# A gated attention and MLP mix on one core: POOL's subtractions go to VectorE, the gelu table is loaded first, a normalisation moves between other products

## The chip, the core and the metric

The kernel runs on one core of a Trainium2 chip. Its engines work side by side, each through its own queue in order: TensorE (PE; its weight loads are listed as PEld), VectorE (DVE), ScalarE (ACT), GpSimd (POOL) and SyncE (SP), which issues most of the DMAs. The metric is the device time of one execution in microseconds (us), lower is better.

## The reference

The input x has 2048 tokens of 448 features, in float32. Two branches are mixed by a gate per token.

```python
g = sigmoid((x * gate_w).sum(-1, keepdims=True))
# A: attention, 16 heads of 28, one k and one v for all heads
q, k, v = x @ wq, x @ wk, x @ wv
o = softmax(q @ k.T * 28 ** -0.5) @ v        # per head
a = o @ wo
# B: MLP
h  = gelu(layernorm(x) @ w1)                 # gelu by tanh
hs = shift(h) @ w2                           # the four quarters of h, shifted by +1, -1, +2, -2 tokens
x1 = x + hs
b  = x1 + gelu(layernorm(x1) @ w3) @ w4      # 448 -> 1792 -> 448
out = g * a + (1 - g) * b
```

## The kernel before

Float32 values are multiplied as two float32r parts: for each weight and activation there is a high part (wh, ah), which ACT makes by a cast, and a low part (wl, al), which is the raw value less the high part. A product takes three matmuls (high by high, high by low, low by high; L115 to L119 in proj). So every matrix that PE reads has had a subtraction made for it on DVE or POOL.

The work is done in blocks of 512 tokens (four blocks, b = 0 to 3), each of four tiles of 128 tokens (t). The stages:

1. Ahead of the MLP. For each block: k, v and the gate's sum from x (stage_kv, stage_v; stage_v transposes vT on PE and DVE copies the result into vext and gz), q for the first two head groups (stage_q), the first layernorm, the w1 product with gelu (stage_w1), the w2 product (stage_w2), which is added to x1. layernorm_stats makes mean and variance by bn_stats on DVE (L126, L127) and rs, the inverse deviation, by two small instructions on POOL (L128, L129). layernorm_tile makes xn on DVE (L135), a pad of 64 columns that repeats its last 64 (L137, on POOL), four transposes on PE (L140), and the split into ah and al (split_a: ACT L109, DVE L110 and L111). In stage_w1 ACT computes gelu twice from PSUM, once into hh (the high part) and once into hf; hl, the low part, is hf less hh, made on POOL (L306). hf has two buffers, xn three, the PSUM tiles mm two, tp two, misc and mx one each.
2. The MLP's weights. load_w34(i), for i = 0 to 6, loads 256 columns of w3 and 256 rows of w4 through one raw buffer each and splits them; the low part of w4 is made on POOL (L371). Before, the first is called ahead of stage_w2(2) and the next three ahead of stage_w2(3). The rest follow behind it.
3. The MLP. Its layernorm of block 0 (ln_begin, ln_tile) lies between the tiles of stage_w2(3); later ones lie within the preceding block. For f = 0 to 13, PE computes 128 columns of w3's product (g), ACT two gelus (gh L409, gf L410), DVE the low part gl (L411), and PE multiplies by w4, two steps later (L419 to L421). DVE adds the sums to x1 (L449).
4. The gate: Exp on ACT (L456), then three small DVE instructions make gg, the gate, and gi, one less the gate.
5. Attention, over 16 units u (four head groups of four token blocks, 16 key tiles kt each, so 256 steps k). Per step there are four score matmuls (L663), four Exps on ACT (L665), and, two steps later, four products with v (L625). Between them lie the q products of later units (q_job), the maxima of scores, the normalisation (norm_job) and the wo products (wo_job), which end in gate_out (L564): out = gg * wo + x1, where x1 has been multiplied by gi on POOL ahead of that (L596, 16 instructions of 128x448).

The order on PE is written out by hand: it runs in the order in which the program issues its instructions (manual_schedule for PE). On the other engines and on the DMA queues a planner orders the instructions when the kernel is built: by its own costs it issues what is ready, in program order among what is ready, and the queue then keeps that order, also where the chip is later or earlier than planned. The planner also places the tables of ACT's functions: a table load (ACT_TABLE_LOAD) comes ahead of an instruction whose function isn't in the table that is loaded.

The lines that the steps of the prediction touch, besides those printed below:

```python
nc.scalar.copy(w4h[i], raw)                                              # L370, ACT
nc.gpsimd.tensor_tensor(w4l[i], raw, f32(w4h[i]), ALU.subtract)          # L371, POOL
stage_w2(NB - 2)                                                         # L386
stage_v(3, vT)                                                           # L387
for i in range(1, 4):
    load_w34(i, s2a)                                                     # L389
ln_tile(0, 0, misc_tile)                                                 # L390
stage_w2(NB - 1, lambda t: ln_tile(0, t + 1, (misc_tile, max_tile)[t % 2]) if t < 3 else None)
```

Of the kernel before, what the change touches and what calls it, by code (L numbers as in the profile page):

```python
# [8 lines left out]
F32 = mybir.dt.float32  # L9
F32R = mybir.dt.float32r  # L10
AF = mybir.ActivationFunctionType
ALU = mybir.AluOpType
# [3 lines left out]
P = 128  # L16
S = 2048
D = 448
# [3 lines left out]
C = D // 4  # L22
NB = S // 512
# [12 lines left out]
def f32(ap):  # L36
    return ap.bitcast(F32)
# [3 lines left out]
def gated_mix_kernel(  # L41
# [33 lines left out]
    sel8 = keep.tile([P, P], F32R, name="sel8")  # L75
    mcs = [keep.tile([P, P], F32R, name=f"mc_{i}") for i in range(2)]
    nc.gpsimd.memset(epst, EPS)
    nc.gpsimd.memset(powt, -0.5)
    nc.gpsimd.memset(vext, 0.0)
# [12 lines left out]
    def misc_tile(name):  # L92
        return psA.tile([P, 512], F32, tag="misc", bufs=1, name=name)

    wps = misc_tile("warm_ps")
    for _ in range(30):
# [35 lines left out]
    def layernorm_tile(pool, tp_of, b, t, mv, rs, ah, al):  # L132
        xt = x1[:, 4 * b + t, :]
        xn = pool.tile([P, 512], F32, tag="xn", bufs=3, name=f"xn_{pool.name}_{b}_{t}")
        nc.vector.tensor_scalar(xn[:, 0:D], xt, mv[:, t, 0:1], rs[:, t:t + 1],  # L135
                                op0=ALU.subtract, op1=ALU.mult)
        nc.gpsimd.tensor_copy(xn[:, D:512], xn[:, 384:D])  # L137
        tp = tp_of(f"tp_{pool.name}_{b}_{t}").rearrange("p (c n) -> p c n", c=4)
        for c in range(4):
            nc.tensor.transpose(tp[:, c, :], xn[:, c * P:(c + 1) * P], ident)  # L140
        cols = slice(t * P, (t + 1) * P)
        split_a(tp, ah[:, :, cols], al[:, :, cols])
# [60 lines left out]
    with tc.tile_pool(name="s1b", bufs=1) as s1b, \  # L203
# [89 lines left out]
        def stage_w1(b):  # L293
# [4 lines left out]
            for m in range(4):  # L298
                ps = mm_tile(f"h_{b}_{m}")
                proj(ps[0:C, :], w1h[:, :, m * C:(m + 1) * C], w1l[:, :, m * C:(m + 1) * C], *acts[b][0:2])  # L300
                if b + 1 < NB:
# [3 lines left out]
                nc.scalar.activation(hf[0:C, :], ps[0:C, :], AF.Gelu_apprx_tanh)  # L305
                nc.gpsimd.tensor_tensor(hl[b][0:C, m, 2:514], hf[0:C, :], f32(hh[b])[0:C, m, 2:514],  # L306
                                        ALU.subtract)
# [23 lines left out]
        vT = stage_kv(0)  # L331
        split_w(wqraw, wqh, wql, nc.gpsimd)
        stage_q(0)
# [3 lines left out]
        for t in range(4):  # L337
            ln1_tile(0, t)
        split_w(w1raw, w1h, w1l, nc.gpsimd)
        stage_w1(0)  # L340
        nc.scalar.copy(w2h[0:C], w2raw[0:C])
        nc.gpsimd.tensor_tensor(w2l[0:C], w2raw[0:C], f32(w2h)[0:C], ALU.subtract)
        stage_w1(1)
# [16 lines left out]
        def load_w34(i, pool):  # L360
# [9 lines left out]
            nc.scalar.copy(w4h[i], raw)  # L370
            nc.gpsimd.tensor_tensor(w4l[i], raw, f32(w4h[i]), ALU.subtract)  # L371

# [7 lines left out]
        def ln_tile(b, t, tp_of):  # L380
            ah, al, mv, rs = acts[b]
            layernorm_tile(s2a, tp_of, b, t, mv, rs, ah, al)

        ln_begin(0)
        load_w34(0, s2a)
        stage_w2(NB - 2)  # L386
        stage_v(3, vT)  # L387
        for i in range(1, 4):
            load_w34(i, s2a)  # L389
        ln_tile(0, 0, misc_tile)  # L390
        stage_w2(NB - 1, lambda t: ln_tile(0, t + 1, (misc_tile, max_tile)[t % 2]) if t < 3 else None)

# [61 lines left out]
    with tc.tile_pool(name="s3", bufs=1, reuse_waits="tile") as s3, \  # L454
            tc.tile_pool(name="ps3", bufs=1, space=PSUM, reuse_waits="tile") as ps3:
        nc.scalar.activation(gg, gz, AF.Exp, scale=-1.0)  # L456
        nc.vector.tensor_scalar(gg, gg, 1.0, None, op0=ALU.add)
# [136 lines left out]

        for n in range(NT):
            nc.gpsimd.tensor_scalar(x1[:, n, :], x1[:, n, :], gi[:, n:n + 1], None, op0=ALU.mult)  # L596

        jobs = []
# [47 lines left out]
        for k in range(NU * NT + LAG):  # L646
# [7 lines left out]
            if k < NU * NT:  # L654
                if kt == (7 if u == 0 else 2) and u + 2 < NU:
                    jobs.insert(0, lambda u=u: q_job(u + 2))
                if kt == 8 and (u + 3) % NG == 0 and u + 3 < NU:
                    load_x((u + 3) // NG)
                p_of[k] = []
                for j in range(4):  # L660
# [149 lines left out]
```

## Time and profile before

| | |
|---|---|
| median of 3 runs | 1070.5 us (1069.8 to 1071.85) |
| profiled execution | 1070.98 us, span 1069.1 us |
| mean granted TensorE clock | 0.987 |
| busy, share of the span | PE 97%, ACT 63%, PEld 64%, DVE 24%, POOL 15% |
| instructions | PE 5610, DVE 521, ACT 1318, POOL 182 |
| table loads on ACT | 5, of 1.283 us each: at 1.19, 26.14, 117.96, 138.38 and 417.95 us |
| stages | up to 132 us: stage 1 and the first weights; 132 to 424: the MLP; from 424: attention |

A row of the timeline gives the start and the duration in us, the engine, the line in the kernel, the operation, what it writes and reads with the shape, how many instructions are merged in it, and in brackets the time that the engine idled before it and what ended that. An x2 row's duration is that of both. Clock shares are those that the throttle granted (1.00 is full speed).

### The profile page before, as it was taken

What the parts mean: (1) busy time and instruction counts of PE and PEld (TensorE: products, weight loads), DVE (VectorE), ACT (ScalarE), POOL (GpSimd) and SP (SyncE); (2) the same over time, 40 slices, a digit from 0 to 9 for tenths busy, and PEclk for the clock granted to TensorE, in tenths of its full rate; (3) what the DMA queues carried; (4) which work ended last, traced back from release to release, by engine and by line L of the source; (5) the groups of instructions that cost most, each with busy time, mean ns of one, the idle gap of its engine ahead of it and who ended that gap; (6) DMA issues with size and microseconds to landing.
All of it is one profiled execution on the core that took longest, in us unless ns stands there. A gap on an engine that the chain in (4) does not pass through costs nothing.

```text
span 1069.1 us, 13948 instructions
## 1 busy us (share of the span) xinstructions
PE 1039.7 (97%) x5610; PEld 679.6 (64%) x5610; DVE 258.0 (24%) x521; ACT 673.2 (63%) x1318; POOL 159.8 (15%) x182
## 2 busy tenths in 40 slices
PE   6999889999999999999999999999999999999995
PEld 4787778888888888454554555554655555555542
DVE  6744952311411311401110110120110210111102
ACT  5444451222222223788888888889888889888873
POOL 5622430110200201603000002010002100000100
PEclk9999899999999999999999999999999999999998
DMA  9401330000000000423211202220202220211001
GB/s 312 131 1 37 111 111 1 1 1 1 1 1 1 1 1 29 164 32 70 33 17 16 31 20 40 39 31 3 39 10 41 39 31 2 40 24 26 10 2 38
DMA packets 30541, 41.15 MB, mean 38 GB/s; under 512 B 8004, under 2 KB 20100, under 8 KB 30340
## 3 DMA queue, kind: packets, MB, share of 16 engines
q1 hardware_dynamic: 30324, 40.04, 16.3%
q8 instruction: 46, 0.75, 0.3%
q14 instruction: 27, 0.22, 0.1%
q10 hardware_dynamic: 144, 0.13, 0.1%
HBM read 23.28 MB, written 3.67 MB: 25 GB/s over the span
## 4 chain that ended last, share of the span: by engine, by line
PE 91%; DVE 4%; DMA 1%; ACT 1%; POOL 1%; issue 1%; SPq 0%; POOLq 0%; ACTq 0%; DVEq 0%
PE s L663 27%; PE pv L625 22%; PE acc L420 4%; PE acc L419 4%; PE acc L421 4%; PE g L115 4%; PE g L116 4%; PE g L117 4%; PE q L503 3%; PE m L166 2%; PE wo L560 1%; PE wo L558 1%; PE wo L556 1%; PE g L119 1%; PE g L118 1%; PE h L116 1%
## 5 line engine op out<-in xcount | busy, mean ns | idle before, releaser
L665 ACT ACTIVATE p<-s 128x512 f32<-128x512 f32 x1024 | 517.6, 627 | 98.1 <-PE s L663 97.8
L663 PE MATMUL s<-qs,kS 98*128 98x512 f32 x1024 | 343.6, 420 | 1.4 <-ACT p L665 0.7
L663 PEld LDWEIGHTS s<-qs,kS 98*128 98x128 f32 x1024 | 181.6, 189 | 168.2 <-ACT p L665 127.1
L625 PE MATMUL pv<-p,vext 128*32 128x512 f32 x2048 | 247.6, 602 | 0.0
L409 ACT ACTIVATE gh<-g 128x512 fp32r<-128x512 f32 x56 | 33.6, 600 | 174.9 <-PE g L119 174.9
L625 PEld LDWEIGHTS pv<-p,vext 128*32 128x32 f32 x2048 | 53.7, 109 | 107.6 <-issue 100.3
L411 DVE TENSOR_TENSOR gl<-gf,gh 128x512 fp32r<-128x512 f32 x56 | 41.3, 738 | 192.1 <-ACT gf L410 192.0
L419 PE MATMUL acc<-w4h,gh 128*128 128x448 f32 x224 | 82.6, 369 | 0.0
L420 PE MATMUL acc<-w4l,gh 128*128 128x448 f32 x224 | 82.0, 366 | 0.0
L421 PE MATMUL acc<-w4h,gl 128*128 128x448 f32 x224 | 81.7, 365 | 0.0
L167 DVE TENSOR_REDUCE mr<-m 128x4 f32<-128x512 f32 x64 | 44.3, 692 | 146.0 <-PE m L166 145.3
L548 POOL CAST onh<-on 128x512 fp32r<-128x512 f32 x15 | 9.2, 614 | 414.8 <-DVE on L545 228.7
L115 PE MATMUL g<-ah,w3h 128*128 128x512 f32 x168 | 67.1, 399 | 3.1 <-ACT gf L410 2.8
L116 PE MATMUL g<-al,w3h 128*128 128x512 f32 x168 | 66.5, 396 | 0.1
L117 PE MATMUL g<-ah,w3l 128*128 128x512 f32 x168 | 66.3, 394 | 0.0
L521 DVE SCALAR_TENSOR_TENSOR good<-rt,good 128x16 f32<-128x16 f32 x15 | 2.6, 175 | 190.2 <-DMA rt<-o 190.2
L419 PEld LDWEIGHTS acc<-w4h,gh 128*128 128x128 f32 x224 | 42.0, 188 | 4.9
L420 PEld LDWEIGHTS acc<-w4l,gh 128*128 128x128 f32 x224 | 42.1, 188 | 4.8
L421 PEld LDWEIGHTS acc<-w4h,gl 128*128 128x128 f32 x224 | 42.0, 188 | 3.6
L166 PEld LDWEIGHTS m<-kS,qs 96*128 96x128 f32 x256 | 38.4, 191 | 6.3 <-DVE mr L167 1.2
L115 PEld LDWEIGHTS g<-ah,w3h 128*128 128x128 f32 x168 | 31.9, 190 | 9.7 <-ACT gf L410 3.3
L564 DVE SCALAR_TENSOR_TENSOR ot<-wo,gg,x 128x448 f32<-128x448 f32 x16 | 10.9, 682 | 108.0 <-PE wo L560 108.0
(204 smaller groups left out, 1144.4 us busy)
## 6 DMA issues: line engine op xcount, KB each, us to landing
qs<-qh SPq DMA_DIRECT2D x32, 256.0 KB
qs<-ql SPq DMA_DIRECT2D x16, 256.0 KB
xq<-in_xT_dram SPq DMA_DIRECT2D x4, 1024.0 KB
x<-in_x_dram SPq DMA_DIRECT2D x4, 896.0 KB
w3raw<-in_w_dram SPq DMA_DIRECT2D x7, 512.0 KB
out_dram<-ot SPq DMA_DIRECT2D x16, 224.0 KB
w4raw<-in_w_dram SPq DMA_DIRECT2D x7, 448.0 KB
xkv<-in_xT_dram SPq DMA_DIRECT2D x3, 1024.0 KB
```

The costliest lines, as they stand in the source:

```text
L115: nc.tensor.matmul(ps, wh[:, c, :], ah[:, c, :], start=(c == 0), stop=False)
L116: nc.tensor.matmul(ps, wh[:, c, :], al[:, c, :], start=False, stop=False)
L117: nc.tensor.matmul(ps, wl[:, c, :], ah[:, c, :], start=False, stop=False)
L166: nc.tensor.matmul(ps[:, j, :], q_of[u][0:96, j, t * P:(t + 1) * P], kS[0:96, 0:MK], start=True, stop=True)
L167: nc.vector.reduce_max(mx_of[u][:, :, t], ps, axis=AX.X)
L411: nc.vector.tensor_sub(gl, gf, f32(gh))
L419: nc.tensor.matmul(ps, gh[:, tok], w4h[i][:, k, :], start=(f == 0), stop=False)
L420: nc.tensor.matmul(ps, gh[:, tok], w4l[i][:, k, :], start=False, stop=False)
L421: nc.tensor.matmul(ps, gl[:, tok], w4h[i][:, k, :], start=False, stop=(f == NF - 1))
L625: nc.tensor.matmul(pv[32 * j:32 * j + 32, :], vext[:, kt, :], ps[j], start=(kt == 0), stop=(kt == NT - 1), tile_position=(0, 32 * j))
L663: nc.tensor.matmul(ps, kS[0:98, kt * P:(kt + 1) * P], q_of[u][0:98, j, :], start=True, stop=True)
L665: nc.scalar.activation(p, ps, AF.Exp, scale=SCALE)
```

## The change

The change has six parts.

- All subtractions that POOL makes ahead of attention go to DVE: the low parts of wq (in two halves of 128 columns), w1, w2, w4, and hl. The pad in layernorm_tile is no longer a copy on POOL; DVE computes it from x1 as a second, 64 columns wide instruction of the same kind as xn's.
- A gelu of four columns is issued on ACT at the start, from a constant tile, so that ACT's first table is gelu's.
- The MLP's layernorm of block 0 lies between the tiles of stage_w2(2) instead of stage_w2(3): stage_v(3) after the first tile, then ln_tile(0, 0) to (0, 2) after the following ones, and ln_tile(0, 3) ahead of stage_w2(3). All use the tp banks instead of misc and mx.
- load_w34(1) to (3) stand behind stage_w2(3) in the program.
- The gate's Exp takes a bias, a zero that DVE computes from x1's last tile (max with 0, then min with 0), so it can't run before x1 is complete.
- The 16 multiplications of x1 by gi stand in unit 1 of the attention, one per key tile, instead of ahead of it.

```diff
@@ kernel's start
+    zero = keep.tile([P, 4], F32, name="zero")
+    nc.gpsimd.memset(powt, -0.5)
     nc.gpsimd.memset(epst, EPS)
-    nc.gpsimd.memset(powt, -0.5)
...
+    nc.scalar.activation(zero, powt, AF.Gelu_apprx_tanh)
     wps = misc_tile("warm_ps")
@@ layernorm_tile
-        nc.vector.tensor_scalar(xn[:, 0:D], xt, mv[:, t, 0:1], rs[:, t:t + 1],
-                                op0=ALU.subtract, op1=ALU.mult)
-        nc.gpsimd.tensor_copy(xn[:, D:512], xn[:, 384:D])
+        for lo, hi, at in ((0, D, 0), (384, D, D)):
+            nc.vector.tensor_scalar(xn[:, at:at + hi - lo], xt[:, lo:hi], mv[:, t, 0:1], rs[:, t:t + 1],
+                                    op0=ALU.subtract, op1=ALU.mult)
@@ stage_w1
-                nc.gpsimd.tensor_tensor(hl[b][0:C, m, 2:514], hf[0:C, :], f32(hh[b])[0:C, m, 2:514],
+                nc.vector.tensor_tensor(hl[b][0:C, m, 2:514], hf[0:C, :], f32(hh[b])[0:C, m, 2:514],
                                         ALU.subtract)
@@ order of the stages
-        split_w(wqraw, wqh, wql, nc.gpsimd)
+        for u in range(2):
+            w = slice(u * P, (u + 1) * P)
+            split_w(wqraw[:, :, w], wqh[:, :, w], wql[:, :, w])
...
-        split_w(w1raw, w1h, w1l, nc.gpsimd)
+        split_w(w1raw, w1h, w1l)
         stage_w1(0)
         nc.scalar.copy(w2h[0:C], w2raw[0:C])
-        nc.gpsimd.tensor_tensor(w2l[0:C], w2raw[0:C], f32(w2h)[0:C], ALU.subtract)
+        nc.vector.tensor_tensor(w2l[0:C], w2raw[0:C], f32(w2h)[0:C], ALU.subtract)
@@ load_w34
-            nc.gpsimd.tensor_tensor(w4l[i], raw, f32(w4h[i]), ALU.subtract)
+            nc.vector.tensor_tensor(w4l[i], raw, f32(w4h[i]), ALU.subtract)
@@ ahead of the MLP
         load_w34(0, s2a)
-        stage_w2(NB - 2)
-        stage_v(3, vT)
+        stage_w2(NB - 2, lambda t: ln_tile(0, t - 1, tp_tile) if t else stage_v(3, vT))
+        ln_tile(0, 3, tp_tile)
+        stage_w2(NB - 1)
         for i in range(1, 4):
             load_w34(i, s2a)
-        ln_tile(0, 0, misc_tile)
-        stage_w2(NB - 1, lambda t: ln_tile(0, t + 1, (misc_tile, max_tile)[t % 2]) if t < 3 else None)
@@ the gate
-        nc.scalar.activation(gg, gz, AF.Exp, scale=-1.0)
+        nc.vector.tensor_scalar(zero[:, 0:1], x1[:, NT - 1, 0:1], 0.0, 0.0, op0=ALU.max, op1=ALU.min)
+        nc.scalar.activation(gg, gz, AF.Exp, scale=-1.0, bias=zero[:, 0:1])
@@ attention
-        for n in range(NT):
-            nc.gpsimd.tensor_scalar(x1[:, n, :], x1[:, n, :], gi[:, n:n + 1], None, op0=ALU.mult)
...
+                if u == 1:
+                    nc.gpsimd.tensor_scalar(x1[:, kt, :], x1[:, kt, :], gi[:, kt:kt + 1], None, op0=ALU.mult)
```

## The prediction

> **What bounds the kernel now.** I read the page's busy rows first (PE busy 97%), then the busy time by stretch, PE's waits up to 170 us, and the timeline around each of those waits. The profiled execution took 1070.98 us (span 1069.1 and 1.9 around it), 0.5 over the median of the runs shown, 1070.5.
>
> The busy time by stretch (columns: length, then PE, PEld, DVE, ACT, POOL busy, PE clock, DMA share, GB/s):
>
> ```profile
> 10.00:42.34 32.34, 23.30 (x102) 16.65 (x102) 27.02 (x64) 16.93 (x27) 21.48 (x29) 0.89 0.96 280
> ...
> 104.58:132.34 27.76, 24.79 (x118) 21.89 (x116) 24.82 (x51) 13.68 (x22) 12.89 (x17) 0.88 0.42 128
> 132.34:147.27 14.93, 12.01 (x45) 9.53 (x46) 8.63 (x16) 9.16 (x15) 8.15 (x10) 0.89 0.48 139
> ```
>
> ```profile
> 170.00:400.00 230.00, 229.76 (x1091) 199.51 (x1090) 54.27 (x98) 55.64 (x103) 21.08 (x23) 1.00 0.00 1
> ```
>
> In the MLP (170 to 400) PE idles 0.24 us in 230: nothing that another engine does there is worth anything. Attention is the same (PE's waits after 425 us add up to under 3 us). What can be won lies in the first three stretches, where PE waits and its granted clock is below 1. PE's longest waits up to 170 us:
>
> ```profile
> PE g L115 <- ACT gf L410: 2.8, 1, 2.8
> PE tp_s2a L140 <- DVE gz L276: 2.7, 1, 2.7
> PE h L116 <- DVE al L110: 1.9, 2, 1.6
> ```
>
> The timeline (start, duration) shows what stands behind them:
>
> ```profile
> 26.47 3.99 POOL L342 TENSOR_TENSOR w2l<-w2raw,w2h 112x1792 fp32r<-112x1792 f32 x1
> 27.10 4.04 DVE L135 TENSOR_SCALAR xn_s<-x,mv_s,rs_s 128x448 f32<-128x448 f32 x2
> ```
>
> ```profile
> 117.96 1.28 ACT L456 ACT_TABLE_LOAD   x1
> 118.02 2.42 POOL L371 TENSOR_TENSOR w4l<-w4raw,w4h 128x896 fp32r<-128x896 f32 x1 [3.71 <-ACT w4h L370]
> 118.42 2.31 DVE L105 TENSOR_TENSOR w3l<-w3raw,w3h 64x256 fp32r<-64x256 f32 x1
> ```
>
> ```profile
> 137.43 0.94 ACT L370 CAST w4h<-w4raw 128x896 fp32r<-128x896 f32 x1 [1.91 <-DMA w4raw<-in_w_dram]
> 138.38 1.28 ACT L409 ACT_TABLE_LOAD   x1
> 139.68 0.60 ACT L409 ACTIVATE gh<-g 128x512 fp32r<-128x512 f32 x1
> 140.17 0.59 ACT L410 ACTIVATE gf<-g 128x512 f32<-128x512 f32 x1
> ```
>
> A DVE instruction on SBUF operands that meets a POOL subtraction ends only when that ends: two of L135, 0.51 each elsewhere, take 4.04; L105, 0.41 elsewhere, takes 2.31. DVE reads of PSUM are not held (L148 at 17.22 took 0.68 beside L104 on POOL). And the gate's Exp (L456), issued in the middle of the gelu work, costs two table loads; the second lies ahead of the first gelu of the MLP, for which PE waits from 138.0 to 140.82.
>
> **Part 1, the first 42 us.** The chain that ended last runs through DVE here (10.99 to 42.34). Added to DVE in this stretch, with durations of its own rows: wq01l in two halves, 128x384 as L110 (0.56) and 64x128 as L111 (0.29); the first half falls into DVE's idle time before 10.99, the second counts, 0.85. w1l: 128x1344 lies between L104 at 768 (0.94) and L110 at 1536 (1.75), 1.55; 64x448 between 0.41 and 0.69, 0.62; together 2.2. w2l at 1792 columns: 2.0, past the last row by the same slope. hl: 0.69 (L411) for three, 2.1. The pads: 128x64 lies between L457 (128x16, 0.15) and L275 (128x112, 0.27), I take 0.19; eight, 1.5. Sum 8.6. Taken away: the stall of L135, 4.04 - 1.02 = 3.0. The remaining 5.6 have two places to go: DVE idles 32.34 - 27.02 = 5.3 here (3.75 of it behind POOL's rs), and 6.9 of its work is ahead of need (eight bn_stats with their aggregates and three xn from 31.06 on, for blocks 2 and 3). PE also loses two waits: q L117 on POOL's wq01l (1.2), which goes over into the wait for vT that follows, so 0; and the transposes behind the pads, which POOL's w1l held from 17.1 to 20.0 (1.0 of PE's time), which go over into DVE's queue. From al at 27.06 to 42.34 PE takes 15.3; at full clock four blocks cost 4 x (11 x 0.231 + 0.44) = 11.9, so at most 3.4 can come out there. I take a gain of 1.0, between 3 gained and 4 lost. The gelu table loaded at once is worth 0: the load that goes (26.14, 1.28) lies in ACT's wait of 3.98 for h, and the first load lies ahead of the first weights (ACT waits for them until 3.90).
>
> From 42 to 104 us PE hardly waits and DVE is busy 26 to 58% of each ten us; thirteen more hl and eight pads (10.5 us) fit. But hf has two buffers: a late hl holds ACT's next hf, and behind that hh, ah and the PSUM bank for h. That is a rival below.
>
> **Part 2, the normalisation between the w2 products.** Before, 104.58 to 132.34 takes 27.76 us. Its matmuls at full clock: 96 of w2 at 0.2035 (19.5), four groups of transposes at 0.44 (1.8), the v transposes 0.3: 21.6. The 6.1 beyond are the wait of 2.7 at 117.77 (the misc bank was held until DVE, late through L135's 3.15 beside POOL's w4l, had copied vp away), 12 matmuls at 0.37 instead of 0.20 after it (2.0), and small ones. With the change vp no longer shares its bank with the transposes, and the fourth transposes have a whole w2 block (9.8 us) behind them before g needs them. New waits: vp now comes after the first token tile, at 107.0, and vT is ready at 107.3 (0.3). The first transposes then come up at 107.6 + 2.44 = 110.1; xn follows rs, which ended at 110.8, so with the pad it is there at 111.6: a wait of 1.5. Behind it stand all of PE's later products. Together 23.4, a gain of 4.4, of which I take off 0.4 for an hl and a w4l ahead of xn in DVE's queue: 4.0 (6 if the statistics come early, 1 if DVE holds xn back for longer).
>
> **Part 3, the start of the MLP.** PE reaches g four us earlier, at 128.3, and ends two blocks (22 x 0.231) at 133.4. It then waits for ACT's gf. In ACT's queue before stands the cast w4h of the fifth weight load ahead of the first gelu (137.43, quoted above), waiting for its transfer; I take that order as kept. That cast is paced by a round: transfer 3.3 to 3.5, w4h 0.94, w4l on POOL 2.1, next transfer (127.54 to 134.01: 6.5). With w4l on DVE, 1.08 by the slope above, a round takes 5.45. From w4l of load 0 ending at 111.6 and a first transfer of 4.1, w4h of load 1 starts at 115.7 and that of load 4 at 132.1, with a us of queueing per two rounds at 133.5. No table load follows; gh and gf end at 135.5, and the third block starts there instead of 140.82: 5.3 earlier in all, 4.0 of it from part 2, 1.3 from here. The wait left is about 2: waits up to 1.6 (vp, 13.8) left the clock at 1, 2.7 and 2.8 did not; the slow matmuls after 140.82 cost 1.4, of which I count half, 0.7. Gain of part 3: 2.0, between 0 and 4.2 (the whole wait and the slow clock).
>
> Beside the load at 138.38 the Trainium skill speaks: its page "ScalarE: Activation LUTs", section "What ACT_TABLE_LOAD costs", puts 1.28 us for the load and another 1.38 for a drain at each switch. The trace shows the load of 1.28 starting 0.01 after the cast's end and gh 0.02 after the load's: no drain. By the page the sum would come out 1.4 lower; I go by the trace.
>
> **Part 4, attention.** The gate's Exp now waits for x1 of the last tile: L449 ends at 424.76, the new max/min on DVE about 0.15 (L457), so at 425.0 the Exp (0.22) can run; the first p starts at 424.38. If it is queued behind the first p it costs 0.3, if ahead of it 0.85; behind it stand all p, which PE waits for until 430. If it is queued later, 0. I take 0.3 lost. The table load stays covered (417.95, 5.1 before the first p). The sixteen products x1 x gi (1.43 each, 22.9) move past POOL's memsets, wql, ahq and onh into the second head group: there POOL has 22.9 + 6.7 (ahq, alq) + 1.9 (onh, onl) = 31.5 of about 39 us; their first reader is gate_out two groups later: 0. The pads in the MLP: 0, its PE never waits.
>
> **Sum:** -1.0 - 4.0 - 2.0 + 0.3 = -6.7 on 1070.98: 1064.3; on the median of the runs, **1063.8**. A measurement of this kernel can tell 0.2%, 2.1 us, from no change.
>
> **Rivals.**
> Gelu first (0.25): the planner puts the first gelu ahead of the late weight casts. For it: PE comes four us earlier. Against: the weights come earlier too, by about the same. Part 3 then gives 4.2: 1061.6.
> Weights ahead (0.15): with rounds of 5.45 one more w4h gets ahead of the first gelu, and the wait grows by a round: 1069.2. For it: ACT's queue before already has one cast out of place.
> Table stays (0.07): the max/min is folded or the Exp is still early, and the load remains at 138.38: 1.3 back, 1065.1.
> DVE becomes the bound (0.08), the slower side: up to 64 us DVE gets 8.6 + five hl (3.4) + four pads (0.8) = 12.8 for 3.0 taken away, and hl stands in the queue ahead of al, through which ACT and PE stall. For it: DVE is busy 27.02 of 32.34 already, and in order. Against: 6.9 of that is ahead of need. If all 9.8 stay on the path: +9.8 - 4.0 - 2.0 + 0.3 = +4.1, 1074.6. It decides from 7.8 us on (5.7 and the 2.1).
>
> **Chances.** Forecast 0.45, the rivals as given. Faster: 0.45 + 0.25 + 0.07 and a third of "weights ahead" with an early gain in part 1, 0.05: 0.82. Within 0.2%: the rest of that one, 0.10. Slower 0.08. The range takes in part 1 at its better end with "gelu first" on the low side (1061.6 - 2, then part 2 at its better end, 1058), and "weights ahead" on the high side, 1069.5.
>
> **What would show it.** Right: no L135 or L105 over 1 us before 424; three table loads (gelu, Exp, at most one more), none between 30 and 400; g starting some 5 us earlier against the first h; PE's wait at the third g block near 2 us, none for gz. Wrong: PE waits for al or hf longer than 2 us between 20 and 60; DVE over 95% busy there; a w4h cast waiting for its DMA ahead of the first gh.

## The result: slower by 1.2%

The changed kernel takes 1084.44 us (median of 4 runs, 1082.79 to 1085.35) against 1071.17 of the kernel before in the same series: ratio 1.0123, interval 1.0104 to 1.0141. The forecast was 1063.8. The profiled execution took 1084.56 us, span 1082.8, 13.7 more than before.

I cut both traces at the same events on PE, so that each part of the prediction has its own row (us; "third w2" is the start of the third block of w2 products, "first acc" of the first product with w4, s and pv are the first scores and the first product with v).

| stretch | before | after | difference | forecast |
|---|---|---|---|---|
| start to third w2 (part 1) | 104.58 | 109.25 | +4.7 | -1.0 |
| third w2 to first g (part 2) | 27.76 | 25.68 | -2.1 | -4.0 |
| first g to first acc (part 3) | 12.51 | 7.52 | -5.0 | -2.0 |
| first acc to first s (the MLP) | 279.09 | 280.02 | +0.9 | 0 |
| first s to first pv | 6.42 | 7.00 | +0.6 | +0.3 |
| first pv to the end of the span | 638.74 | 653.33 | +14.6 | 0 |
| sum | | | +13.7 | -6.7 |

One row decides the sign. PE's longest waits over the whole span, after the change:

```profile
PE q L507 <- POOL alq L493: 12.1, 1, 12.1
PE vp L275 <- ACT vT L269: 3.1, 1, 3.1
PE h L118 <- DVE al L112: 3.0, 2, 1.8
PE tp_s2a L142 <- DVE xn_s2a L138: 2.6, 2, 2.4
```

The wait of 12.1 did not exist before, nor is there a wait for gf at the third g any more. What POOL did meanwhile stands in its timeline after the change:

```profile
424.72 11.29 POOL L661 TENSOR_SCALAR x<-x,gi 128x448 f32<-128x448 f32 x7 [7.86 <-DVE gi L463]
435.98 1.84 POOL L586 TENSOR_TENSOR wql<-wqraw,wqh 128x768 fp32r<-128x768 f32 x1
...
440.96 8.31 POOL L661 TENSOR_SCALAR x<-x,gi 128x448 f32<-128x448 f32 x6
449.23 3.42 POOL L493 TENSOR_TENSOR alq<-xq,ahq 128x1536 fp32r<-128x1536 f32 x1
```

Thirteen products of x1 and gi (L661) run ahead of alq, the low part of the x that the q product of unit 2 reads. In the kernel before, twelve of the sixteen ran inside the MLP, in fours from 211.57, 282.95 and 354.34; the other four ran between 423.03 and 430.27, and none stood between wql and alq:

```profile
423.03 2.79 POOL L596 TENSOR_SCALAR x<-x,gi 128x448 f32<-128x448 f32 x2 [62.91 <-DVE x L449]
...
427.48 2.79 POOL L596 TENSOR_SCALAR x<-x,gi 128x448 f32<-128x448 f32 x2
...
437.35 3.49 POOL L489 TENSOR_TENSOR alq<-xq,ahq 128x1536 fp32r<-128x1536 f32 x1 [1.32 <-DVE ahq L488]
```

So alq ran at 437.35 before and runs at 449.23 now. PE's order is fixed, and from 440.6 on it stands at that q. The same stretch by tens of us (length, PE, PEld, DVE, ACT, POOL busy, PE clock, DMA share, GB/s):

```profile
430.00:440.00 10.00, 10.00 (x52) 4.55 (x45) 2.48 (x4) 6.86 (x15) 10.00 (x7) 0.79 0.00 0
440.00:450.00 10.00, 0.59 (x3) 0.15 (x1) 0.10 (x1) 2.34 (x5) 10.00 (x9) 0.72 0.28 92
450.00:460.00 10.00, 7.29 (x32) 3.85 (x33) 0.73 (x2) 1.60 (x4) 9.82 (x7) 0.60 0.32 107
```

POOL is busy for ten of ten us and PE for 0.59 from 440 to 450. In the ten us in which PE resumes (at 452.7) its clock is 0.60: a group of 16 pv takes 3.64 at 454.18 and took 1.92 at 435.93. Of the 14.6 us the wait is 12.1; the slow clock around it is the likely home of the other 2.5 (an estimate: the granted clock is 0.58 from 452.7 to 459.0, and 6.3 x 0.42 is 2.6).

The first three stretches after the change (same columns):

```profile
10.00:42.34 32.34, 24.58 (x100) 17.91 (x98) 28.14 (x69) 14.66 (x25) 4.18 (x5) 0.79 0.99 278
109.25:134.93 25.68, 22.65 (x118) 19.78 (x117) 22.22 (x51) 11.67 (x20) 2.52 (x8) 1.00 0.42 140
134.93:142.45 7.52, 7.52 (x34) 6.19 (x33) 6.75 (x16) 4.26 (x8) 1.77 (x4) 1.00 0.42 136
```

In the first, POOL fell from 21.48 to 4.18 us, DVE rose by only 1.1, and the clock fell from 0.89 to 0.79. In the second and third the clock is now 1.00 (before, 0.88 and, up to 147.27, 0.89), and the third has no idle PE at all: the start of the MLP went better than forecast.

### The profile page after: what moved, and what is told of

Same layout as the page of the kernel before. It is cut to its first block, busy times and chain, and to the rows that moved or that the text cites. A ratio compares the mean times of both kernels' runs of the same rounds, so it can differ in the third digit from the quotient of the medians.

```text
span 1082.8 us, 13947 instructions
## 1 busy us (share of the span) xinstructions
PE 1042.7 (96%) x5610; PEld 680.8 (63%) x5610; DVE 275.5 (25%) x584; ACT 670.5 (62%) x1319; POOL 109.8 (10%) x123
## 4 chain that ended last, share of the span: by engine, by line
PE 89%; DVE 3%; DMA 2%; POOL 2%; ACT 2%; issue 0%; SPq 0%; DVEq 0%; ACTq 0%; POOLq 0%
PE s L666 26%; PE pv L626 22%; PE acc L422 4%; PE acc L423 4%; PE acc L424 4%; PE g L117 3%; PE g L118 3%; PE g L119 3%; PE q L507 3%; PE m L168 2%; PE wo L564 1%; PE wo L562 1%; PE wo L560 1%; PE g L121 1%; PE g L120 1%; DMA w1raw<-in_w_dram 1%
## 5 line engine op out<-in xcount | busy, mean ns | idle before, releaser
L414 DVE TENSOR_TENSOR gl<-gf,gh 128x512 fp32r<-128x512 f32 x56 | 38.6, 692 | 179.6 <-ACT gf L413 179.5
L168 PE MATMUL m<-kS,qs 96*128 96x128 f32 x256 | 36.4, 265 | 0.4 <-DVE mr L169 0.4
```

Of the source, the lines that this page charges most:

```text
L168: nc.tensor.matmul(ps[:, j, :], q_of[u][0:96, j, t * P:(t + 1) * P], kS[0:96, 0:MK], start=True, stop=True)
L414: nc.vector.tensor_sub(gl, gf, f32(gh))
```

## Experiments on attention: what puts the products first

In the kernel before, 12 of the 16 products had run inside the MLP. The change did two things to them: it wrote them later (in unit 1), and it held the gate's Exp, so that gi is made only at 424.35. The first experiment writes them ahead of attention again and keeps the held Exp.

```diff
@@ a1_loop_back: from the changed kernel
+        for n in range(NT):
+            nc.gpsimd.tensor_scalar(x1[:, n, :], x1[:, n, :], gi[:, n:n + 1], None, op0=ALU.mult)
...
-                if u == 1:
-                    nc.gpsimd.tensor_scalar(x1[:, kt, :], ...)
```

> The changed kernel, with the 16 products x1 * gi written ahead of attention again, as in the kernel before. Theory H (the gate's Exp, held until x1 is complete, makes all 16 products ready at once at attention's start, and the planner fills POOL's waits with them, wherever the program writes them): POOL's queue stays the same, PE waits about 12 us for alq near 440, total 1084.5 +- 1.5. Theory W (writing them into unit 1 is what put them there): the wait goes, total about 1070.

Measured: 1086.22 us, ratio 1.0129 (1.0108 to 1.0151), PE's wait for alq 14.1: theory H, with a total a little above its range. From the first pv to the end it takes 653.3 us, as long as the changed kernel, so where the products are written makes no difference to attention; the total is longer because third w2 to first g takes 28.0 here. The second takes the hold from the Exp and leaves the products in unit 1.

```diff
@@ a2_exp_early: from the changed kernel
-        nc.scalar.activation(gg, gz, AF.Exp, scale=-1.0, bias=zero[:, 0:1])
+        nc.scalar.activation(gg, gz, AF.Exp, scale=-1.0)
```

> The changed kernel with the gate's Exp free again (no zero as its bias); the products x1 * gi stay in unit 1. Theory H: most of the 16 products are done within the MLP, no PE wait for alq over 1 us, attention 14 us shorter; the Exp goes back into the gelu work with two table loads, which costs 0 to 4 us at the MLP's start: total 1070 to 1074. Theory W: the wait for alq stays, total 1084 or more.

Measured: 1070.37 us, ratio 0.9985 (0.9971 to 0.9999); the wait for alq is 1.4 (theory H: under 1), the table loads are back at 112.73 and 136.67, and first s to first pv is 6.4 again. The third keeps the held Exp and makes gi wait for the maxima of unit 1 (they are multiplied by zero and added), so the products can't be ready when POOL still has alq to do.

```diff
@@ a3_gi_late: from the changed kernel, in unit 1 at kt == 0
+                        nc.vector.tensor_scalar(gi, gg, -1.0, 1.0, op0=ALU.mult, op1=ALU.add)
+                        nc.vector.scalar_tensor_tensor(gi, late_of[1], 0.0, gi, op0=ALU.mult, op1=ALU.add)
```

> The changed kernel with gi made to wait for the score maxima of unit 1 (gi gets 0 times the maxima added), so that the products are ready only some 30 us into attention. The Exp stays held. Theory H: no PE wait for alq, all 14 us come back, total 1070 +- 1 and attention's first score matmul at about 422.5 as in the changed kernel. Rival: POOL's wql and alq are late for another reason (casts on VectorE, the transfer): PE still waits some us there, total over 1074.

Measured: 1069.69 us, ratio 0.9981 (0.9968 to 0.9994). POOL's timeline of this kernel:

```profile
436.04 3.47 POOL L494 TENSOR_TENSOR alq<-xq,ahq 128x1536 fp32r<-128x1536 f32 x1 [1.31 <-ACT p L672]
...
442.69 4.06 POOL L598 TENSOR_TENSOR wol<-woraw,woh 128x1792 fp32r<-128x1792 f32 x1
447.49 22.12 POOL L665 TENSOR_SCALAR x<-x,gi 128x448 f32<-128x448 f32 x16 [0.74 <-DVE gi L664]
```

All 16 follow alq, woh and wol, and PE waits for none of them. So the loss of some 15 us is the meeting of two things: the held Exp makes all 16 products of 1.43 ready at the start of attention, and the planner, which takes what is ready, puts thirteen of them ahead of alq. That the hold does it is shown by the three runs; why the planner took thirteen is not. On the chip DVE had made wqh and ahq by 431.98, and wql and alq are 8.6 us of work on POOL; by an estimate they could have ended near 440.5, where PE comes to its q. The order was fixed before that by the planner's own costs, which no run shows. Everything below is built on a3_gi_late, so that attention is out of the way.

## Experiments on the first 105 us: four moves that do not add

First each of the four moves to DVE was undone alone, then all four together. For these kernels I count from the first q product, because that start varies by up to a us between executions; the columns split at the first transposes (tp) of the first layernorm.

```diff
@@ b1_wq_pool
+        split_w(wqraw, wqh, wql, nc.gpsimd)          # in place of two halves on DVE
@@ b2_w12_pool
+        split_w(w1raw, w1h, w1l, nc.gpsimd)
+        nc.gpsimd.tensor_tensor(w2l[0:C], w2raw[0:C], f32(w2h)[0:C], ALU.subtract)
@@ b3_hl_pool
+                nc.gpsimd.tensor_tensor(hl[b][0:C, m, 2:514], hf[0:C, :], ...
@@ b4_pad_pool
+        nc.gpsimd.tensor_copy(xn[:, D:512], xn[:, 384:D])   # in place of the second DVE instruction
@@ b5_all_pool: all four (w4l stays on DVE, the normalisation where the change has it)
```

> As the one with gi late, and the low part of wq back on POOL in one piece; the rest of stage 1 stays on VectorE. Theory C (the earlier wq part only made PE end its first q product sooner, so that its wait for vT grew from 1.6 to 3.2 us, over the point at which the clock is lowered, and the second q product ran slow): the wait for vT is 1.6 to 2.0 again, the first transposes start near 18.3 instead of 19.3 to 20.5, and the third w2 block starts 1 to 2 us before the 108.9 of the one with gi late. Rival Q (VectorE's queue alone sets this stage): 0 to 0.8 us earlier.

> As the one with gi late, and the low parts of w1 and w2 back on POOL (4.2 us less on VectorE). Theory Q (VectorE's queue): the third w2 block starts 1 to 3 us before 108.9. Rival S (they cost VectorE as much on POOL, by holding its instructions: 3 us before): no more than 0.7 us earlier.

> As the one with gi late, and hl back on POOL. Theory Q: 2.8 us less on VectorE in each block of stage 1; the first h of the second block waits under 1.2 us for al instead of 2, without the slow clock after it, and the third w2 block starts 1.5 to 3 us before 108.9. Rival (hl is done in VectorE's waits): under 0.7 us earlier.

> As the one with gi late, and the pads back on POOL. Theory Q: 0.2 to 0.3 us less on VectorE for each of them, eight up to the second block: the third w2 block starts 0.5 to 2 us before 108.9. Between the w2 products the first transposes' wait for the pad (2.4) shrinks to about 1.2, since on POOL the pad isn't queued behind w3l and w4l: another 1.2 us. Rival (the pads lie in waits): no gain before 109.

> As the one with gi late, and besides that all of stage 1 back on POOL: low parts of wq (in one piece), w1, w2, hl and the pads; w4's low part stays on VectorE, and the new order of the normalisation too. Theory D (VectorE's longer queue cost the 4.7 us up to 109 us of the changed kernel): the third w2 block starts at 104.6 +- 0.7 again, total 1065 to 1067. If the pads on POOL hold the transposes between the w2 products, 1 to 2 us of that are lost. Rival (the loss there comes from the gelu table at the start or from the order of the DMAs): the third w2 block stays at 109, total 1070.

Then the reverse: one move alone on DVE, the other three on POOL (b5_all_pool with one of the edits above taken out).

```diff
@@ d1_wq_dve: b5_all_pool without b1's edit      d2_w12_dve: without b2's
@@ d3_hl_dve: without b3's                       d4_pad_dve: without b4's
```

> b5_all_pool with the one move of wq01l (two halves of 128x384 and 64x128) to DVE; w1l, w2l, hl and the pads stay on POOL. In b5_all_pool the third w2 block starts at 104.58, with all four moves on DVE (a3_gi_late) at 108.90. Theory 'own time': each move costs its share of those 4.3 us by its DVE time of part 1 (0.85 of 8.6): third block at 105.0. Theory 'gap and clock': q of unit 0 ends earlier while vT does not, PE waits about 3 for vT, its clock falls, and the first transposes start near 20.5 instead of 18.1: 2.3 later, of which DVE's queue, without the other three moves, gives little back: third block at 106 to 107. Theory 'filled queue': a single move falls into DVE's idle time: 104.6. Total time 1066.6 plus the same difference.

> b5_all_pool with w1l and w2l on DVE, the rest of part 1 on POOL. Theory 'own time': 4.2 of 8.6, so 2.1 later: third block at 106.7. Theory 'filled queue': DVE is given 4.2 us of its own and rid of the 3.0 in which POOL's w2l held two xn, 1.2 net, and its 5.3 us of idle time takes that: 104.6, or up to 1 earlier (103.6), since the pads no longer lie behind POOL's w1l, which cost PE 1.0 before. Theory 'gap and clock': PE's wait for vT stays at 1.6 and the transposes start at 18.1: nothing is lost before the first h.

> b5_all_pool with hl on DVE, the rest of part 1 on POOL. Theory 'own time': 2.1 of 8.6 up to 42 us, 1.1 later: third block at 105.6. Theory 'filled queue': 2.1 us fall into 5.3 of idle time: 104.6. Theory 'filled queue, with holds': hl stands on DVE ahead of al of the next block, and POOL's pads and w2l hold it; each hl held for one POOL operation costs up to 1 us: 106 to 107 and PE waits for al at h.

> b5_all_pool with the pads on DVE, the rest of part 1 on POOL. Theory 'own time': 1.5 of 8.6 up to 42 us, 0.75 later: third block at 105.3. Theory 'filled queue': the pads fall into idle time, and the transposes no longer wait for the pads behind POOL's w1l (1.0 of PE's time before): 103.6 to 104.6. In part 2, where b5_all_pool takes 24.9 from the third w2 block to the first g, a pad of token tile 0 queued on DVE behind w3l and w4l would add up to 0.8 (25.7).

| kernel | on DVE | q to tp | tp to third w2 | both | ratio to before (interval) |
|---|---|---|---|---|---|
| before | none | 8.89 | 86.20 | 95.1 | 1 |
| b5_all_pool | none | 8.82 | 86.46 | 95.3 | 0.9959 (0.9943 to 0.9976) |
| a3_gi_late | all | 10.40 | 89.56 | 100.0 | 0.9981 (0.9968 to 0.9994) |
| b1_wq_pool | all but wq | 8.84 | 91.01 | 99.9 | 0.9988 (0.9971 to 1.0004) |
| b2_w12_pool | all but w1, w2 | 11.65 | 92.08 | 103.7 | 1.0019 (1.0005 to 1.0033) |
| b3_hl_pool | all but hl | 11.63 | 91.13 | 102.8 | 1.0016 (0.9995 to 1.0037) |
| b4_pad_pool | all but pads | 11.61 | 88.48 | 100.1 | 0.9999 (0.9988 to 1.0011) |
| d1_wq_dve | wq | 9.76 | 85.85 | 95.6 | 0.9949 (0.9935 to 0.9963) |
| d2_w12_dve | w1, w2 | 9.89 | 89.91 | 99.8 | 1.0002 (0.9988 to 1.0015) |
| d3_hl_dve | hl | 8.86 | 87.50 | 96.4 | 0.9961 (0.9944 to 0.9979) |
| d4_pad_dve | pads | 10.39 | 94.50 | 104.9 | 1.0038 (1.0022 to 1.0054) |

All four together cost 4.7; alone they cost 0.3, 4.5, 1.1 and 9.6, in sum 15.5; and undoing any one of them gives nothing back. One trace stands behind each row, so small differences need a measure. Six kernels have none of the four on DVE (before, b5_all_pool and the four others of the next section): they take 95.1 to 95.7. Four have all of them there (the changed kernel, a1, a2 and a3): 98.8 to 100.2, with a first column of 8.3 to 11.3. So the 0.3 of wq can't be told from nothing, and the 1.1 of hl hardly; in total time, too, d1 and d3 are level with b5_all_pool. "Own time" fails for w1 and w2 and for the pads, and so does the theory that a single move falls into DVE's idle time (it holds for wq and nearly for hl alone). Where the cost is large, it is in who stands beside whom and ahead of whom. In b2_w12_pool, DVE and then POOL:

```profile
15.89 5.36 DVE L138 TENSOR_SCALAR xn_s<-x,mv_s,rs_s 128x448 f32<-128x448 f32 x5 [1.44 <-POOL rs_s L131]
...
31.40 5.70 DVE L138 TENSOR_SCALAR xn_s<-x,mv_s,rs_s 128x448 f32<-128x448 f32 x6 [1.41 <-POOL rs_s L131]
```

```profile
15.82 3.05 POOL L106 TENSOR_TENSOR w1l<-w1raw,w1h 128x1344 fp32r<-128x1344 f32 x1
...
31.33 4.00 POOL L348 TENSOR_TENSOR w2l<-w2raw,w2h 112x1792 fp32r<-112x1792 f32 x1
```

Five xn and pads, 1.80 elsewhere, take 5.36 because POOL's subtraction began 0.07 earlier. With the pads on POOL, as in b5_all_pool, POOL has a pad to copy ahead of w1l, and w1l starts at 16.50, when the first three xn are nearly done (15.52 to 16.88). d4_pad_dve has the same rows of 5.36 and 5.69 as b2_w12_pool, and PE's waits of 4.2 and 4.1 behind them. The Trainium skill, page "SBUF — State Buffer", section "SBUF: two separate sides", calls the port pair that DVE and GpSimd share "an exclusive lock, not a bandwidth split", held by the first for its whole instruction. These rows agree (POOL's two pieces of w1l end at 20.13, the five on DVE at 21.25), and so does the other direction: POOL's rs, 0.20 alone, took 1.89 at 29.15 after the change, beside DVE's w2l of 1.99 at 28.98. The forecast looked at only one direction.

d2_w12_dve has no xn held by POOL and loses 4.5 all the same. (It has one hold the other way, three pads on POOL that take 2.52 at 16.89 beside w1l on DVE; that may be part of its longer first column.) DVE and then POOL:

```profile
17.59 1.55 DVE L106 TENSOR_TENSOR w1l<-w1raw,w1h 128x1344 fp32r<-128x1344 f32 x1
...
29.68 0.18 DVE L129 BATCH_NORM_AGGREGATE mv_s<-st_s 128x2 f32<-128x6 f32 x1
...
34.44 1.36 DVE L137 TENSOR_SCALAR xn_s<-x,mv_s,rs_s 128x448 f32<-128x448 f32 x3 [3.55 <-POOL rs_s L131]
```

```profile
32.06 1.09 POOL L310 TENSOR_TENSOR hl<-hf,hh 112x512 fp32r<-112x512 f32 x1 [7.70 <-ACT hf L309]
33.10 0.20 POOL L130 TENSOR_TENSOR rs_s<-mv_s,epst 128x4 f32<-128x4 f32 x1
```

Here w1l goes ahead of the second block's statistics (L128, L129), and w2l (27.77, 1.99) ahead of the last of them; they end at 29.9 instead of 24.0, and rs, which needs them, is queued on POOL behind an hl that waits until 32.06 for hf. rs ends nine us later than in b5_all_pool, and DVE idles 3.55 for it. After the change the same chain is late without that queue: rs starts at 29.15 (24.29 before). s1_stats_first tests it by issuing those statistics ahead of w1's split.

```diff
@@ s1_stats_first: from a3_gi_late
+        ln1_begin(1)
         split_w(w1raw, w1h, w1l)
         stage_w1(0)
...
-            if b + 1 < NB:
+            if 0 < b < NB - 1:
                 ln1_begin(b + 1)
```

> a3_gi_late (everything of part 1 on DVE) with one change: the statistics of the second block of tokens are issued ahead of the split of w1, so DVE's queue has them before w1l. In a3_gi_late the third w2 block starts 99.96 after the first q product, in b5_all_pool 95.28; the inverse deviation of the second block starts on POOL at 27.82 and 24.05. Theory 'late statistics' (w1l pushes the second block's statistics back, and behind them xn, transposes, ah and al of that block): the inverse deviation starts near 25.5, and 2 to 3 of the 4.7 us come back: 97 to 98. Theory 'DVE is full' (what moves ahead only pushes w1l and the first h back): no more than 1 comes back: 99 to 100. Theory 'gap and clock' (PE's wait of 3.1 for vT slows the first 40 us): as 'DVE is full'; the wait stays at 3.

Measured: 97.4 (10.80 and 86.64), ratio 0.9965 (0.9951 to 0.9980): 2.5 of the 4.7 came back (1.7 by the ratios of the total), though rs started only at 26.86, held for 1.42. PE's wait for vT stayed (3.3). Behind the first transposes nothing is left to explain: 86.64 against 86.46. The last of this series moves w2l alone.

```diff
@@ s2_w2_dve: from b5_all_pool
+        nc.vector.tensor_tensor(w2l[0:C], w2raw[0:C], f32(w2h)[0:C], ALU.subtract)
```

> b5_all_pool with w2l alone on DVE; w1l stays on POOL. In d2_w12_dve, with both on DVE, the third w2 block came 99.80 after the first q product against 95.28 (the second block's inverse deviation at 33.10, queued on POOL behind an hl that waits for hf). Theory 'late statistics': the statistics are done before w2l starts, the inverse deviation stays near 24.1, and two xn are no longer held (4.04 for two of 0.51) for 2.0 of DVE: 94 to 95.5. Theory 'own time': 2.0 of 8.6, 1.0 later: 96.3. Theory 'POOL in order': the planner puts the inverse deviation behind hl here as well: 98 to 100.

Measured: 97.7 (10.65 and 87.04), ratio 0.9983 (0.9971 to 0.9995). rs started at 25.37, 5.0 after tp (5.9 in b5_all_pool), so the statistics were not late, but two pads on POOL now took 2.50 beside DVE's w2l; and the first column is 1.8 longer for a reason that is not w2l: its q products ran at 0.63 us each from 13.1 on, after a wait of only 1.23. The gain that the theory of the statistics allowed (up to 1.3) did not come; the run can't say more, since its clock differed.

What is left of part 1, some 2 us, lies before the first transposes. There the changed kernel gives PE, with wq01l on DVE, a longer wait and then slow products:

```profile
15.11 0.63 PE L275 MATMUL vp<-ident,vT 32*128 32x32 f32 x4 [3.15 <-ACT vT L269]
...
16.26 0.63 PE L118 MATMUL q<-alk,wq01h 128*128 128x512 f32 x1
```

The same q products took 0.40 each in b5_all_pool, where PE had waited 1.6. b1_wq_pool, with wq on POOL again, has the first column back (8.84), and d1_wq_dve has lost 0.9 of it; b1_wq_pool then loses as much in the second column. But the slow products do not always come: a2_exp_early, with the same four moves, has them at 0.40 after a wait of 2.66, and a first column of 8.32. Nor is a low clock a loss by itself: e1_old_order (next section) has 0.79 from 10 to 42.34, as the changed kernel has, and takes 95.6. So these 2 us are argued from the traces and not shown; both causes removed at once was not tried.

## Experiments on the start of the MLP

b5_all_pool differs from the kernel before in four things: w4l on DVE, the normalisation's place, the gelu table with the held Exp, and late products. These kernels take them apart (on b5_all_pool).

```diff
@@ e1_old_order: b5_all_pool with the normalisation and load_w34(1) to (3) at their places of before
         stage_w2(NB - 2)
         stage_v(3, vT)
         for i in range(1, 4):
             load_w34(i, s2a)
         ln_tile(0, 0, misc_tile)
         stage_w2(NB - 1, lambda t: ln_tile(0, t + 1, (misc_tile, max_tile)[t % 2]) if t < 3 else None)
@@ e2_exp_early: b5_all_pool with the unheld Exp
@@ f1_table_only: e1_old_order with
+            nc.gpsimd.tensor_tensor(w4l[i], raw, f32(w4h[i]), ALU.subtract)
@@ f2_w4_only: e1_old_order with the unheld Exp
```

> b5_all_pool with the old place of the MLP's first normalisation (between the tiles of the last w2 product, in the misc and mx banks, and the weight loads 1 to 3 ahead of it). w4l stays on DVE, the gelu table loaded once. Third w2 block to first g: 24.88 in b5_all_pool, 27.76 in the kernel before. Theory 'the order gives it': 27.5 to 28, PE's wait of 2.7 for gz is back, total 1069 to 1069.7. Theory 'the hold gave it' (w4l on POOL held xn, and the old order is as good without that hold): 25 to 26, total 1066.6 to 1067.5.

> b5_all_pool with the gate's Exp without the held bias, so it can run among the gelus, as before the change; the 16 products of x1 and gi stay behind the first maxima. Theory 'two loads on the path': a load of 1.28 lies ahead of the first gelu of the MLP again, first g to first acc grows from 7.53 to 8.8 to 9.4, and attention's start is 0.3 to 0.6 earlier: total 1067.2 to 1068.2. Theory 'weights pace it' (the fourth g waits 2.0 for gelu behind the w4h casts anyway): the load falls into that wait: 1066.0 to 1066.8.

> e1_old_order with w4l back on POOL: of the whole change only the gelu table loaded first and the held Exp are left (with the 16 products behind the first maxima). In e1_old_order the third w2 block to the first g takes 23.61, first g to first acc 7.52, total 1062.97. Theory 'the hold gave it' (DVE's xn held by w4l on POOL, and through it the bank that the transposes need): PE waits 2.7 for gz again, 27.5 to 28; the first gelus no longer wait for a table load, first g to first acc 8 to 11; total 1066 to 1069. Theory 'the table gave it' (the load among the gelus was what cost time, w4l is indifferent): 23.6 to 24.5 and a total of 1063 to 1064.

> e1_old_order with the gate's Exp unheld: of the whole change only w4l on DVE is left (and the products of x1 and gi behind the first maxima). Theory 'the hold gave it': third w2 block to first g 23.6 to 24.5, as in e1_old_order; one table load of 1.28 lies ahead of the first gelu of the MLP, PE waits 1.5 to 4 there, total 1064 to 1066. Theory 'the table gave it': 27 to 28 to the first g, total 1068 or more.

| kernel | w4l | place | table loads in it | third w2 to g | g to acc | median, us | ratio (interval) |
|---|---|---|---|---|---|---|---|
| before | POOL | old | 2 | 27.76 | 12.51 | 1071.84 | 1 |
| f1_table_only | POOL | old | 0 | 27.90 | 10.65 | 1070.51 | 0.9997 (0.9978 to 1.0017) |
| f2_w4_only | DVE | old | 2 | 24.64 | 13.29 | 1068.70 | 0.9976 (0.9954 to 0.9997) |
| e1_old_order | DVE | old | 0 | 23.61 | 7.52 | 1062.97 | 0.9922 (0.9906 to 0.9939) |
| b5_all_pool | DVE | new | 0 | 24.88 | 7.53 | 1066.57 | 0.9959 (0.9943 to 0.9976) |
| e2_exp_early | DVE | new | 2 | 23.54 | 13.09 | 1068.39 | 0.9968 (0.9956 to 0.9980) |

(The median of before is that of e1_old_order's series; in the others it was 1071.46 and 1071.70.) "The hold gave it" is right for part 2. With w4l on POOL three xn of the first token tiles take 3.16 at 111.64 in f1_table_only, beside POOL's w4l (111.58, 2.13). That row of DVE, and PE's waits of that kernel in this stretch:

```profile
111.64 3.16 DVE L137 TENSOR_SCALAR xn_s2a<-x,mv_s2a,rs_s2a 128x448 f32<-128x448 f32 x3
...
PE g L118 <- DVE al L112: 2.7, 1, 2.7
PE tp_s2a L142 <- DVE gz L280: 2.7, 1, 2.7
```

With w4l on DVE, in e1_old_order, at the same old place:

```profile
PE tp_s2a L142 <- DVE gz L280: 0.7, 1, 0.7
PE tp_s2a L142 <- DVE ah L113: 0.7, 1, 0.7
```

```profile
104.97:128.58 23.61, 22.25 (x118) 19.79 (x117) 21.17 (x46) 12.21 (x21) 6.33 (x13) 1.00 0.49 144
128.58:136.10 7.52, 7.52 (x34) 6.19 (x33) 6.55 (x13) 4.67 (x9) 1.88 (x5) 1.00 0.54 161
```

The wait of 2.7 for gz shrinks to 0.7 with w4l alone, and the slow clock is gone. With the held Exp the new place is worse by 1.3 there (b5_all_pool against e1_old_order), and by 2.0 at the fourth g block, where b5_all_pool's ACT and then PE show:

```profile
137.58 0.83 ACT L103 CAST w3h<-w3raw 128x768 fp32r<-128x768 f32 x1 [3.57 <-DMA w3raw<-in_w_dram]
...
140.15 0.94 ACT L374 CAST w4h<-w4raw 128x896 fp32r<-128x896 f32 x1 [0.38 <-DMA w4raw<-in_w_dram]
140.99 0.59 ACT L413 ACTIVATE gf<-g 128x512 f32<-128x512 f32 x1
```

```profile
141.63 0.50 PE L117 MATMUL g<-ah,w3h 128*128 128x512 f32 x1 [2.03 <-ACT gf L413]
```

The second block's gf is queued behind a w4h cast that waits for its transfer. In e1_old_order the fifth w3 cast comes at 134.09, 3.5 earlier, the queue has the same order, and PE idles 0.3 there. (e1_old_order also issues load_w34(1) to (3) earlier; the two were not separated.) With the free Exp it is the other way round up to the first g: 23.54 at the new place (e2_exp_early), 24.64 at the old one (f2_w4_only). So the runs show no gain or loss that belongs to the place alone. The new place with w4l on POOL was not run.

f1_table_only and f2_w4_only show that the two improvements need each other: by the ratios the table alone gives 0.3 us (not distinguishable from none), w4l alone 2.6, both 8.4. With w4l alone PE reaches g 3 us earlier and waits it out behind the load (a wait of 3.3 for gf; the clock from first g to first acc is 0.79); with the table alone, g waits for al, which DVE, held, has late. I had expected 1064 to 1066 for f2_w4_only and 1066 to 1069 for f1_table_only: both were slower than that, while e1_old_order was faster than either theory had it (25 to 26 and 1066.6 at best). e2_exp_early came out 1.8 slower than b5_all_pool by the medians (1.0 by the ratios), so the load does not simply fall into the wait.

e1_old_order, that is the kernel before with w4l on DVE, the gelu table first with the held Exp, and the products of x1 and gi behind the first maxima, is the fastest of these versions: 1062.97 us.

## Why the prediction was wrong, step by step

**Part 4 is the step that failed.** It said that the sixteen products "move past POOL's memsets, wql, ahq and onh into the second head group" and priced that at 0. The stretch behind the first pv lost 14.6, of which 12.1 is PE's wait for alq behind thirteen of these products. Only their place in the program moves there. POOL's order is the planner's, by readiness, and the rows of before already said so: twelve of the same products stood in the MLP although the program wrote them behind wol. The prediction counted POOL's room over 39 us (31.5 of it used) and never asked what is ready first and who waits for the last. The held Exp was priced for ACT alone, 0.3 (0.6 measured between s and pv), while its result releases 23 us of POOL work at the start of attention. No rival had this case.

**Part 1 was mis-sized: -1.0 against +4.7, outside its own range of 3 gained to 4 lost.** The single prices were right (w1l 1.55 and 0.61, w2l 1.99, hl 0.69). The term that failed is where the remaining 5.6 should go: into 5.3 of DVE's idle time and into 6.9 of work "ahead of need". That work is of blocks 2 and 3 and stands at the end of the stretch, from 31.06 on; the added subtractions stand ahead of something else, the statistics of the second block, b = 1 (17.88 to 24.21 before), which were not ahead of need. Behind w1l these pushed rs from 24.29 to 29.15, and that was worth 2.5 (s1_stats_first). Room was counted as a sum, without the order in the queue. And q's wait on wq01l that "goes over into the wait for vT that follows, so 0" did go over, 1.6 to 3.1, but the products behind it then ran at 0.63 instead of 0.40 each (not in a2_exp_early). "DVE becomes the bound" was the nearest rival for this part, with a chance of 0.08; but it named hl ahead of al, which alone cost 1.1 at most, and its full price of 9.8 did not occur.

**Part 2 was half right in size (-2.1 against -4.0, inside its range of 1 to 6) and credited to an edit that was not needed for it.** The prediction itself named the cause, "late through L135's 3.15 beside POOL's w4l", and then put the gain on the new place. At the old place w4l on DVE alone took 27.90 to 23.61 (f1_table_only to e1_old_order), and with it there the new place was worse by 1.3 or better by 1.1. What the new place would give with w4l on POOL stays open. The forecast's wait for xn (1.5) became 2.4, since the pad of the first tile (117.89) stood behind w3l, an x addition and w4l in DVE's queue.

**Part 3 came out at its far end and beyond.** First g to first acc lost 5.0, the whole wait and the slow clock; the load at 138.38 is gone as predicted, and the changed kernel has two loads in all, at 1.18 and 416.48. The weight rounds of 5.45 were wrong: the w3 casts are 8.57, 6.89, 7.28 and 6.84 apart after the change (8.65, 7.53, 6.26 and 7.96 in b5_all_pool). After the change that did not matter, because g came later than forecast by 6.6 us (134.93 for 128.3). So part of the gain is luck: in b5_all_pool, where g comes at 129.46, PE does wait the 2.0 of the forecast, one g block later.

The signs that the prediction gave for right and wrong were half useful: no held xn, no load among the gelus and no wait for gz all came true. But g was not 5 us earlier against the first h (108.34 behind it, 107.88 before), none of the signs of being wrong appeared, and the wait that decided lay in a stretch that it had dismissed in one sentence ("PE's waits after 425 us add up to under 3 us").

## What to carry to other kernels

When an operand is made to arrive late, list everything that it releases, on every engine, and what else that engine has to do just then: a planner that fills idle queues takes the ready work, not the urgent work. When work moves between DVE and POOL, price the chain that runs through both (statistics, rs, xn) rather than the sum of busy time, and undo edits in groups, for single undoings can all come out worse. And where a wait is explained by a neighbour that holds an engine, try first to remove the neighbour alone.

## What the runs showed of the chip that I had not expected

DVE and POOL hold each other in both directions, and up to the whole of the other's instruction: rs on POOL 1.89 instead of 0.20 beside w2l on DVE, two pads 2.50 instead of 0.66 or less, five xn and pads on DVE 5.36 instead of 1.80. The prediction's sentence that a DVE instruction on SBUF operands is held was too general: in the kernel before, two bn_stats took 1.14 at 17.88 beside POOL's w1l (16.75 to 20.06), and 1.15 at 25.54 after the change, where POOL stood still.

PE's clock falls after short gaps, but no fixed length of the gap decides. After the change a wait of 3.15, from 12.0 to 15.1, was followed by products of 0.63. In a2_exp_early, with the same order up to there, a wait of 2.66, up to 15.12, was followed by products of 0.40. The wait of about 1.23 for wq01l, which every kernel with wq on POOL has, was followed by products of 0.40 in the kernel before and in b5_all_pool and by 0.63 in six others (s2_w2_dve and e1_old_order among them). The wait of 2.4 for xn after the change left its stretch (from 109.25) at 1.00. The Trainium skill, page "TensorE: Matmul & The Clock Gate", section "What's actually happening", gives an idle window of about 3.4 us that runs freely, so that the point of change depends on where in the window the first matmul lands. That a gap's place counts besides its length fits these runs; 3.4 us as the least idle time does not, since here 1.23 and 3.15 were enough. What share of idle time in a window decides, no run here shows.
